# A planner that lets GpSimd and VectorE's SBUF-only operations take turns

## The chip, the cores and the metric

The kernel runs on one core of one Trainium2 chip. The core has five engines with a queue of instructions each: TensorE (PE in the profile, its weight loads PEld), VectorE (DVE), ScalarE (ACT), GpSimd (POOL) and SyncE (SP), from whose queue all DMAs of this kernel are issued. Each engine works through its own queue in order; between engines there are only semaphores. The metric is device time in microseconds (us) of one execution; less is better.

## The reference

A delta-rule linear attention over 4 batches, 8 heads, 768 positions and head width 48, and behind it a gated MLP with a mix over the sequence:

```python
k_n = k / (np.linalg.norm(k, axis=-1, keepdims=True) + 1e-06)
for t in range(S):
    y[:, :, t] = einsum('bhd,bhde->bhe', q[:, :, t], state)
    v_old = einsum('bhde,bhd->bhe', state, k_n[:, :, t])
    state += beta_t * outer(k_n[:, :, t], v[:, :, t] - v_old)
...
h = relu(x @ w_in); u, v = halves of h        # x: 4 x 768 x 384, d_ff 1024
v_n = (v - mean(v)) / sqrt(var(v) + 1e-06)
v_s = w_spatial @ v_n + b_spatial
out = (u * v_s) @ w_out
```

Some weights of the MLP arrive as 64-bit floats and are taken apart into 32-bit words on the chip.

## The kernel before, in words

**The work.** The sequence is cut into chunks of 64 positions; 4 batches of 12 chunks make 48 *steps*. A step computes, for four pairs of heads at a time, in matmuls of 64 rows or fewer (the "tiles", all issued at L438): `a` (state times keys), `b` (the chunk's triangular inverse times the corrected values, whose result VectorE scales into the tile `us`, L795), `c` (the state's update, added at L823), `qk` (masked at L839) and `d` (the output, copied out by ScalarE at L868). Each step's `b` needs the step before it of the same batch.

Steps come in 12 groups of four. For a group, `norm` makes the coefficients `cn` from the keys' squares (VectorE, L557 to L583), `mask` scales a mask by them (GpSimd, L595; on VectorE for two chunks), `kk` makes the triangular matrices (VectorE L630 into `ta`), a DMA through DRAM puts them into another layout (`ad`, `la`), and `lanes` inverts 32x32 blocks with 60 VectorE operations (L670 and L677, on the tile `pw` in PSUM) before another DMA brings them back; `step_t` and `step_ef` put the blocks together. The first group goes a shorter way, `lanes16` (L1181, L1188, all in SBUF).

**The MLP.** When four steps of a batch are done, `convert` splits their output into a high and a low part for fp32r matmuls: ScalarE writes `xh` (L911), GpSimd or, late in the kernel, VectorE subtracts to get `xl` (L915). Then follow the tasks `v` (L946), `u` (L1012), `g` (L1044, the mix over the sequence) and `o` (L1099) on TensorE with their work on the other engines; `vl` (L992) and `gl` (L1086) are low parts as `xl` is. `post_v` has six small VectorE operations on the tile `sm` (helper `small`, L963 to L983).

**The weights.** `load_w` loads a piece of a weight, and where it holds 64-bit floats six VectorE operations on SBUF (L467 to L483, tile `wstage` or `ub`) and one on GpSimd (L485) make 32-bit floats of it; ScalarE (L487) and GpSimd (L489) make the high and the low part. The pieces of `w_in` are needed before the first `v`, those of `w_spatial` and `w_out` before the first `g`.

**What sets the order.** Every engine's queue is written by a planner, the class `Line`, while the kernel is built. Every job is a generator that yields one operation at a time: an engine, how long it holds that engine (`occ`), when its result is there (`lat`), a condition, and a due time. `step` collects the operations that can begin, finds the earliest, takes those of the same engine that could begin almost as early (within `SLACK`), and emits the one whose due time is first. VectorE's costs come from `dve`, GpSimd's from `pool`. Where TensorE would stand still in the plan, `keep_warm` puts in filler matmuls (L1282, tile `ones`), and `tensor` lets two tile operations of different kinds (the kinds "anti" and "diag") run interleaved in one *round*; a round with no partner is run alone, or beside a filler on the tile `mpos`. So a changed cost or condition in the planner can change every queue of the program, and the count of fillers and lone rounds with it. The planner's times are used nowhere on the chip: what holds an instruction there is its place in the queue, its semaphores, and the hardware.

## Time and profile before

| | us |
|---|---|
| median of 3 executions (range) | 556.83 (556.48 to 558.57) |
| the profiled execution, its own time | 559.02 |
| its span, first to last instruction | 557.3 |
| TensorE busy | 509.1 (91%) |
| VectorE busy | 355.2 (64%) |
| ScalarE busy | 216.9 (39%) |
| GpSimd busy | 140.7 (25%) |
| mean granted TensorE clock | 0.941 |

Lines (L...) are those of the kernel before. A row of the timeline gives start, duration, engine, line, operation, the tile written and the tiles read, shapes and count; in brackets how long the engine had nothing to do before, and who ended that. A row of the chain of waits gives start, duration and what the chain stands in. Matmul times are modelled as pipelined, so that TensorE's share is no share of its peak; fillers count as busy.

### The profile page before, as it was taken

To read this page: it belongs to the slowest core of one execution; us is meant where nothing else is said; L and a number is where in the kernel's file an instruction comes from. 1 tells how busy PE (TensorE), PEld (TensorE's weight loads), DVE (VectorE), ACT (ScalarE), POOL (GpSimd) and SP (SyncE) were. 2 spreads that over 40 slices of the span, in tenths; PEclk is the share of its full clock that TensorE was granted. 3 is DMA by queue.
4 is the path that set the end of the run, shared out by engine and by line. 5 is a ranking of instruction groups with operands and counts; after the bars stand their busy time and mean duration, and the time that the engine had idled before them with its cause. 6 is when DMAs were issued, how large, how long until landed. Compare 5 with 4: busy or idle time off the path is not lost.

```text
span 557.3 us, 22530 instructions
## 1 busy us (share of the span) xinstructions
PE 509.1 (91%) x9605; PEld 460.0 (83%) x9605; DVE 355.2 (64%) x1436; ACT 216.9 (39%) x536; POOL 140.7 (25%) x210
## 2 busy tenths in 40 slices
PE   5965797978979999899999999999999999999997
PEld 5855786867867879798987789989987999999997
DVE  4899978776977988478989894683135241134210
ACT  3222524544625535242235465422165441137111
POOL 5525224555425441402314252310001000000000
PEclk9777586897999999899999999999999999999999
DMA  8688378495759754786875727343014010100011
GB/s 241 163 179 163 88 186 220 113 259 104 181 158 191 187 135 91 177 219 146 204 133 79 204 73 173 112 142 62 29 35 133 8 36 29 35 18 16 1 42 44
DMA packets 134256, 67.03 MB, mean 120 GB/s; under 512 B 105894, under 2 KB 123532, under 8 KB 134156
## 3 DMA queue, kind: packets, MB, share of 16 engines
q1 hardware_dynamic: 134156, 65.60, 47.8%
q8 instruction: 75, 1.23, 0.9%
q14 instruction: 25, 0.20, 0.1%
HBM read 50.11 MB, written 15.17 MB: 117 GB/s over the span
## 4 chain that ended last, share of the span: by engine, by line
PE 65%; DVE 16%; DMA 7%; issue 4%; ACT 3%; SPq 3%; POOL 0%; DVEq 0%; ACTq 0%
PE pt L438 22%; PE pm L1044 12%; PE pw L1044 6%; PE pm L1012 6%; PE pm L946 5%; PE pm L1099 5%; PE pw L1099 3%; DVE prod L670 3%; DVE pw L677 3%; DMA kv<-in_kv_t 2%; DMA la<-ad 2%; PE pm L1282 2%; PE pw L946 2%; PE pw L1012 1%; DMA ad<-ta 1%
## 5 line engine op out<-in xcount | busy, mean ns | idle before, releaser
L670 DVE TENSOR_TENSOR prod<-pw,la 128x96 f32<-128x96 f32 (+10 forms) x330 | 78.3, 241 | 13.4 <-ACT pw L664 8.8
L677 DVE TENSOR_TENSOR pw<-pw,prod 128x96 f32<-128x96 f32 (+9 forms) x330 | 81.1, 249 | 4.6
L719 POOL TENSOR_TENSOR kv<-kv,cn 128x192 f32<-128x192 f32 x48 | 24.9, 519 | 159.4 <-DMA kv<-in_kv_t 93.1
L1044 PE MATMUL pm<-wsp_h,vh 128*128 128x256 f32 x192 | 57.0, 297 | 0.0
L1044 PE MATMUL pm<-wsp_l,vh 128*128 128x256 f32 x192 | 54.2, 282 | 0.6 <-issue 0.6
L1044 PE MATMUL pm<-wsp_h,vl 128*128 128x256 f32 x192 | 54.0, 281 | 0.0
L438 PE MATMUL pt<-kv,st 48*64 48x64 f32 x768 | 53.8, 232 | 0.0
L438 PE MATMUL pt<-aq,us 64*64 64x64 f32 x768 | 52.0, 227 | 0.8 <-issue 0.8
L438 PEld LDWEIGHTS pt<-kv,st 48*64 48x64 f32 x768 | 43.3, 142 | 3.2 <-DVE ta L630 1.5
L1080 ACT CAST gh<-tmp 128x512 fp32r<-128x512 f32 x24 | 14.8, 619 | 76.0 <-DVE tmp L1061 76.0
L438 PEld LDWEIGHTS pt<-aq,us 64*64 64x64 f32 x768 | 43.5, 142 | 1.0 <-issue 1.0
L1282 PE MATMUL pm<-ones 128*128 128x256 f32 x215 | 40.6, 339 | 3.2 <-ACT ones L282 2.5
L438 PE MATMUL pt<-ta,pi 64*64 64x32 f32 x768 | 36.2, 235 | 5.1 <-issue 3.9
L595 POOL TENSOR_TENSOR mc<-mpos,cn 128x256 f32<-128x256 f32 x46 | 28.3, 628 | 43.1 <-DVE cn L583 24.8
L438 PE MATMUL pt<-kv 48*64 48x64 f32 x768 | 36.0, 233 | 3.2 <-issue 2.2
L438 PEld LDWEIGHTS pt<-kv,ta 64*64 64x64 f32 x768 | 30.2, 145 | 9.8 <-issue 3.2
L438 PEld LDWEIGHTS pt<-st,kv 48*64 48x64 f32 x704 | 26.9, 141 | 13.8 <-issue 3.7
L1282 PEld LDWEIGHTS pm<-ones 128*128 128x128 f32 x215 | 33.8, 231 | 5.3 <-ACT ones L282 2.5
L868 ACT ACTIVATE xs<-pt 112x256 f32<-112x256 f32 x48 | 18.3, 381 | 50.7 <-PE pt L438 40.1
L1044 PEld LDWEIGHTS pm<-wsp_h,vh 128*128 128x128 f32 x192 | 36.4, 190 | 1.6
L438 PE MATMUL pt<-kv,ta 64*64 64x48 f32 x768 | 35.9, 233 | 1.9 <-DVE kv L779 0.5
L1044 PEld LDWEIGHTS pm<-wsp_h,vl 128*128 128x128 f32 x192 | 36.6, 190 | 0.6 <-issue 0.6
(182 smaller groups left out, 1488.2 us busy)
## 6 DMA issues: line engine op xcount, KB each, us to landing
kv<-in_kv_t SPq DMA_DIRECT2D x48, 456.0 KB, 4.5
ad<-ta SPq DMA_DIRECT2D x24, 256.0 KB, 4.5
la<-ad SPq DMA_DIRECT2D x44, 128.0 KB, 4.1
out<-ob SPq DMA_DIRECT2D x24, 192.0 KB, 1.9
k<-in_kv_t SPq DMA_DIRECT2D x20, 224.0 KB, 3.6
knn<-in_k_nat SPq DMA_DIRECT2D x10, 384.0 KB, 3.9
wd<-w SPq DMA_DIRECT2D x22, 128.0 KB, 3.9
ta<-wd SPq DMA_DIRECT2D x44, 64.0 KB, 3.5
```

The lines of the kernel that those rows point to most:

```text
L438: return lambda: nc.tensor.matmul(*a, **dict(dict(start=True, stop=True), **k))
L595: (nc.vector if t in (0, 2) else nc.gpsimd).tensor_tensor(out=mc, in0=mall, in1=cns[t // G][:, t % G, 1].unsqueeze(2).broadcast_to([128, N ...
L670: nc.vector.tensor_tensor(out=pr, in0=w[:, :n, j : j + 1].broadcast_to([128, n, m]), in1=la[:, j, j + 1 : 32].unsqueeze(1).broadcast_to([1 ...
L677: nc.vector.tensor_add(out=w[:, :n, j + 1 : 32], in0=w[:, :n, j + 1 : 32], in1=pr)
L719: nc.gpsimd.tensor_tensor(out=v, in0=v, in1=cns[s // G][:, s % G, 0].unsqueeze(2).broadcast_to([128, NU, HD]), op=ALU.mult)
L868: nc.scalar.mul(out=xt[0:112, :, qt * 64 : qt * 64 + 64], in_=psl(held[0][1], CH)[0:112], mul=-1.0)
L946: nc.tensor.matmul(p[1], a[:, kt, ts], w[:, kt, DH:], start=(n == 0), stop=(n == 3 * NK - 1))
L1012: nc.tensor.matmul(pu[:, k], w[:, kt, d0 : d0 + 128], a[:, kt], start=(n == 0), stop=(n == 3 * NK - 1))
L1044: nc.tensor.matmul(pg[:, k], v[:, d0 : d0 + 128], w[:, si, ts], start=(n == 0), stop=False)
L1080: nc.scalar.copy(out=gh[:, hs], in_=gt)
L1099: nc.tensor.matmul(p[1][:, :DM], a[:, dd, ts], w[:, dd], start=(n == 0), stop=(n == 3 * ND - 1))
L1282: nc.tensor.matmul(free[0].rearrange("p (n t) -> p n t", t=128), ones, ones.unsqueeze(1).broadcast_to([128, 2, 128]), start=True, stop=True,)
```

## The change

The planner gets two more clocks, `held["DVE"]` and `held["POOL"]`. A VectorE operation made by the new helper `dve_sb` is of the kind "port". In the plan such an operation does not begin before the last planned GpSimd operation has ended, and no GpSimd operation begins before the last planned "port" operation has ended. All other VectorE operations are planned as before. No instruction gets a new wait on the chip, none moves to another engine; VectorE has 1436 instructions in both versions, ScalarE's, GpSimd's and SyncE's counts are the same too, and TensorE's differ by fillers alone.

```diff
@@ class Line
+        self.held = {"DVE": 0.0, "POOL": 0.0}
...
             if t is not None:
-                found.append((max(self.t[op.eng], t), op, j, t))
+                e = max(self.t[op.eng], t)
+                if op.eng == "POOL":
+                    e = max(e, self.held["DVE"])
+                elif op.kind == "port":
+                    e = max(e, self.held["POOL"])
+                found.append((e, op, j, t))
...
         t, op, j, _ = min(near, key=lambda f: (f[1].due(), f[0]))
+        t = self.port(op, t)
         self.t[eng] = t + op.occ
         self.grant(j, t + op.lat)
+
+    def port(self, op, t):
+
+        if op.eng == "POOL":
+            t = max(t, self.held["DVE"])
+            self.held["POOL"] = t + op.occ
+        elif op.kind == "port":
+            t = max(t, self.held["POOL"])
+            self.held["DVE"] = t + op.occ
+        return t
...
+def dve_sb(dep, due, e, fast=1.0):
+
+    op = dve(dep, due, e, fast)
+    op.kind = "port"
+    return op
...
-            t = yield dve(on(t), d, n, 0.5)
+            t = yield dve_sb(on(t), d, n, 0.5)
             nc.vector.tensor_scalar(
                 out=e, in0=w1, scalar1=20, scalar2=0x7FF, op0=ALU.logical_shift_right, op1=ALU.bitwise_and
             )
```

The same replacement of `dve` by `dve_sb` is made for all six operations of `load_w`, for the square at L557 and L569, L573, L575, L577, L581, L583 of `norm` (not for its sums and reciprocals), for the two masks on VectorE (L595), for `lanes16` (L1181, L1188, L1190) and for L1254. The operations of `small`, `xl`, `vl` and `gl` where VectorE does them, and everything that reads or writes PSUM stay `dve`.

Lines behind the new code stand 24 higher in the changed file. Three places show what the new plan makes of the queues.

VectorE's queue around the fifth step's `us` (L795; L819 in the changed file), where `norm` makes the coefficients of the fifth group. Before:

```order
L795 TENSOR_TENSOR us<-pt,cs 128x192
L562 TENSOR_REDUCE ss<-knn 128x8
L670 TENSOR_TENSOR prod<-pw,la 128x120
L569 TENSOR_SCALAR t<-nr 128x16
L677 TENSOR_TENSOR pw<-pw,prod 128x10x12
L571 RECIPROCAL t<-t 128x16
```

And in the changed program, where that step's `us` is the instruction 33 places ahead of L593:

```order
L847 TENSOR_TENSOR st<-st,pt 112x192
L701 TENSOR_TENSOR pw<-pw,prod 128x13x6
L701 TENSOR_TENSOR pw<-pw,prod 128x2x27
L694 TENSOR_TENSOR prod<-pw,la 128x65
L593 TENSOR_SCALAR t<-nr 128x16
L701 TENSOR_TENSOR pw<-pw,prod 128x13x5
L595 RECIPROCAL t<-t 128x16
```

The first of the coefficient operations (L569, now L593) stood three instructions behind the fifth step's `us` and now stands 33 behind it.

VectorE's queue around the tenth step's `us`. Before:

```order
L677 TENSOR_TENSOR pw<-pw,prod 128x15
L779 TENSOR_TENSOR kv<-kv,pt 128x192
L682 MEMSET pw 64x16
L839 TENSOR_TENSOR aq<-pt,mpos 128x256
L682 MEMSET pw 64x16
L467 TENSOR_SCALAR wstage<-wstage 128x256
L471 TENSOR_SCALAR wstage<-wstage 128x256
L795 TENSOR_TENSOR us<-pt,cs 128x192
L473 TENSOR_SCALAR wstage<-wstage 128x256
```

And now:

```order
L701 TENSOR_TENSOR pw<-pw,prod 128x15
L819 TENSOR_TENSOR us<-pt,cs 128x192
L706 MEMSET pw 64x16
L863 TENSOR_TENSOR aq<-pt,mpos 128x256
L706 MEMSET pw 64x16
L847 TENSOR_TENSOR st<-st,pt 112x192
L605 TENSOR_TENSOR t<-nr,ball 128x16
L863 TENSOR_TENSOR aq<-pt,mpos 128x256
L607 SCALAR_TENSOR_TENSOR cn<-t,nr 128x4x4
L491 TENSOR_SCALAR wstage<-wstage 128x128
L491 TENSOR_SCALAR wstage<-wstage 128x256
```

Two operations on a weight piece (L467 and L471; L491 and L495 now) stood ahead of the step's `us`; now they stand behind it and behind the state's update.

TensorE's queue around the tenth step, with buffer numbers; a row that ends in x8 is a round of eight small matmuls with no partner, and alternating rows are a round of two operations. Before:

```order
L438 MATMUL pt1_204<-ta2_179,pi0_91 64x32 x8
L438 MATMUL pt2_205<-st1_110,kv0_167 64x48
L438 MATMUL pt3_206<-ta2_179,pi1_92 64x32
...
L438 MATMUL pt0_203<-kv1_168 64x64 x8
L1282 MATMUL pm0_207<-ones_67 128x256 x6
```

And now:

```order
L462 MATMUL pt2_205<-ta2_179,pi0_91 64x32 x8
L462 MATMUL pt0_203<-kv0_167 64x64 x8
L462 MATMUL pt1_204<-st1_110,kv0_167 64x48
L462 MATMUL pt3_206<-tn1_176,ta2_179 64x32
...
L462 MATMUL pt2_205<-kv1_168 64x64 x8
L1306 MATMUL pm0_207<-ones_67 128x256
L462 MATMUL pt0_203<-ta2_179,pi1_92 64x32 x8
L462 MATMUL pt3_206<-kv0_167,ta2_179 64x48 x8
```

The last block product of the group (`ta2,pi1`) shared a round with the state's update (`st1,kv0`) and now runs alone, as do two more. Over the whole program there are 236 rounds before and 239 now; those of eight matmuls with no partner are 60 before and 70 now. Filler matmuls on `ones` are 253 before and 247 now, those on `mpos` 232 and 200.

More of the change, by code (lines that the diff above doesn't have):

```diff
@@ L469, in load_w @@
             )
-            t = yield dve(on(t), d, n, 0.5)
+            t = yield dve_sb(on(t), d, n, 0.5)
             nc.vector.tensor_scalar(out=e, in0=e, scalar1=896.0, scalar2=1150.0, op0=ALU.max, op1=ALU.min)
-            t = yield dve(on(t), d, n, 0.5)
+            t = yield dve_sb(on(t), d, n, 0.5)
             nc.vector.tensor_scalar(
@@ L475, in load_w @@
             )
-            t = yield dve(on(t), d, n)
+            t = yield dve_sb(on(t), d, n)
             nc.vector.scalar_tensor_tensor(
@@ L555, in norm @@
             if g == 0:
-                t = yield dve(on(t), d, n)
+                t = yield dve_sb(on(t), d, n)
                 nc.vector.tensor_mul(out=kp, in0=kp, in1=kp)
@@ L567, in norm @@
         n3 = nr.rearrange("p (s u) -> p s u", u=NU)
-        t = yield dve(on(t), d, 16)
+        t = yield dve_sb(on(t), d, 16)
         nc.vector.tensor_scalar_max(out=t0, in0=nr, scalar1=1e-30)
@@ L571, in norm @@
         nc.vector.reciprocal(out=t0, in_=t0)
-        t = yield dve(on(t), d, 16)
+        t = yield dve_sb(on(t), d, 16)
         nc.vector.tensor_mul(out=t0, in0=t0, in1=ss)
-        t = yield dve(on(t), d, 16)
+        t = yield dve_sb(on(t), d, 16)
         nc.vector.tensor_add(out=t0, in0=t0, in1=nr)
-        t = yield dve(on(t), d, 16)
+        t = yield dve_sb(on(t), d, 16)
         nc.vector.tensor_scalar(out=cn[:, :, 0], in0=t3, scalar1=0.5, scalar2=EPS, op0=ALU.mult, op1=ALU.add)
@@ L579, in norm @@
         nc.vector.reciprocal(out=n3, in_=cn[:, :, 0])
-        t = yield dve(on(t), d, 16)
+        t = yield dve_sb(on(t), d, 16)
         nc.vector.tensor_mul(out=t3, in0=n3, in1=bn)
-        t = yield dve(on(t), d, 16)
+        t = yield dve_sb(on(t), d, 16)
         nc.vector.scalar_tensor_tensor(out=cn[:, :, 1], in0=t3, scalar=-1.0, in1=n3, op0=ALU.mult, op1=ALU.mult)
@@ L593, in mask @@
         dep = at(("cn", t // G), ("kk", t - 2) if t >= 2 else None)
-        x = yield dve(dep, d, 256) if t in (0, 2) else pool(dep, d, 256)
+        x = yield dve_sb(dep, d, 256) if t in (0, 2) else pool(dep, d, 256)
         (nc.vector if t in (0, 2) else nc.gpsimd).tensor_tensor(
@@ L1179, in lanes16 @@
             pr = pt[:, : j * m].rearrange("p (a b) -> p a b", b=m)
-            t = yield dve(on(t), d, j * m)
+            t = yield dve_sb(on(t), d, j * m)
             nc.vector.tensor_tensor(
@@ L1186, in lanes16 @@
             )
-            t = yield dve(on(t), d, j * m)
+            t = yield dve_sb(on(t), d, j * m)
             nc.vector.tensor_add(out=w[:, :j, j + 1 : 16], in0=w[:, :j, j + 1 : 16], in1=pr)
-        t = yield dve(on(t), d, 16)
+        t = yield dve_sb(on(t), d, 16)
         nc.vector.memset(w.rearrange("p i t -> p (i t)")[:, 0:256:17], 1.0)
@@ L1252, in load_bias @@
         nc.scalar.copy(out=brow[r], in_=x[r])
-        t = yield dve(on(t), due(4), 256)
+        t = yield dve_sb(on(t), due(4), 256)
         nc.vector.scalar_tensor_tensor(
```

4 lines of the change are left out of this document (2 added, 2 removed).

## The prediction

> **What bounds the kernel now.** I first read the busy times in four stretches.
>
> ```profile
> core 0: us, PE busy (x) PEld busy (x) DVE busy (x) ACT busy (x) POOL busy (x), PEclk, DMA share, GB/s
> 0.00:63.00 63.00, 43.11 (x964) 39.41 (x966) 52.52 (x194) 20.92 (x59) 27.74 (x69) 0.77 0.74 172
> 63.00:200.00 137.00, 120.47 (x2953) 104.60 (x2951) 110.74 (x500) 62.42 (x163) 61.44 (x77) 0.88 0.70 174
> 200.00:380.00 180.00, 172.65 (x3814) 153.62 (x3815) 141.08 (x611) 74.45 (x184) 48.98 (x60) 0.99 0.61 144
> 380.00:557.30 177.30, 172.91 (x1883) 162.39 (x1881) 50.84 (x134) 59.14 (x132) 2.53 (x5) 1.00 0.12 36
> ```
>
> From 200 us on TensorE is busy for 345.6 of 357.3 us, at a full clock: there the end moves only with TensorE's own work. Before 200 us TensorE is idle for 36.4 us, part of the rest is fillers, and VectorE is busy for 163.3 of 200 us (82%). So time can be won before 200 us, on VectorE's queue and on the waits between engines, and what is won there shifts the TensorE-bound part forward. GpSimd is busy for 89.2 us of these 200, so it is often in the way if it can be in the way at all. Whether it can, two places of the timeline show.
>
> ```profile
> 90.84 0.36 DVE L795 TENSOR_TENSOR us<-pt,cs 128x192 f32<-128x192 f32 x1
> 93.96 1.81 POOL L915 TENSOR_TENSOR xl<-xs,xh 128x768 fp32r<-128x768 f32 x1 [3.37 <-ACT xh L911]
> 94.29 1.52 DVE L569 TENSOR_SCALAR t<-nr 128x16 f32<-128x16 f32 x1 [2.45 <-ACT nr L564]
> 96.84 0.17 DVE L577 TENSOR_SCALAR cn<-t 128x16 f32<-128x16 f32 x1
> ...
> 133.21 1.83 POOL L915 TENSOR_TENSOR xl<-xs,xh 128x768 fp32r<-128x768 f32 x1 [2.91 <-ACT xh L911]
> 134.34 0.85 DVE L467 TENSOR_SCALAR wstage<-wstage 128x256 uint32<-128x256 uint32 x1
> 135.73 0.34 DVE L795 TENSOR_TENSOR us<-pt,cs 128x192 f32<-128x192 f32 x1
> 136.46 0.42 DVE L477 SCALAR_TENSOR_TENSOR wstage<-wstage 128x256 uint32<-128x256 uint32 x1
> ...
> 19.98 0.28 DVE L481 TENSOR_SCALAR wstage<-wstage 128x256 uint32<-128x256 uint32 x1
> ```
>
> L569 works on 16 elements, for which its like (L577) takes 0.17 us. It took 1.52 us and ended at 95.81, just behind GpSimd's subtraction, which ended at 95.77. L467 at 134.34 took 0.85 us where an undisturbed operation of that size takes 0.28 (L481), and the `us` of the tenth step stood behind it. So a VectorE operation on SBUF that finds a GpSimd operation under way waits for its end, with everything queued behind it. How much that is in all, the groups by shape show.
>
> ```profile
> L569 DVE TENSOR_SCALAR t<-nr 128x16 f32<-128x16 f32 x12 | 5.4, 448 | 3.1 <-ACT nr L564 2.7
> L467 DVE TENSOR_SCALAR wstage<-wstage 128x256 uint32<-128x256 uint32 x14 | 5.7, 410 | 0.5 <-DMA wstage<-in_w_in 0.5
> L477 DVE SCALAR_TENSOR_TENSOR wstage<-wstage 128x256 uint32<-128x256 uint32 x14 | 7.1, 510 | 0.0
> L481 DVE TENSOR_SCALAR wstage<-wstage 128x256 uint32<-128x256 uint32 x14 | 5.5, 395 | 0.0
> L471 DVE TENSOR_SCALAR wstage<-wstage 128x256 uint32<-128x256 uint32 x14 | 4.9, 352 | 0.1
> L977 DVE SCALAR_TENSOR_TENSOR sm<-sm 128x1 f32<-128x1 f32 x24 | 6.5, 272 | 0.4
> L983 DVE TENSOR_TENSOR sm<-sm 128x1 f32<-128x1 f32 x24 | 5.9, 248 | 0.4
> L630 DVE TENSOR_TENSOR ta<-pt,mc 128x256 f32<-128x256 f32 x48 | 19.7, 414 | 2.4 <-PE pt L438 1.6
> ```
>
> L569 lost 12 x (448 - 170) = 3.3 us, L467 14 x (410 - 280) = 1.8, L477 14 x (510 - 420) = 1.3, L481 1.6 and L471 1.0 in the same way. Counted instruction by instruction (VectorE beside a running GpSimd instruction, more than 60 ns over the usual time of its own shape) 52 instructions lost 20.8 us. Of that 17.2 us fell on operations that the change marks as "port", and 3.6 on L977 and L983, which it doesn't mark. L630, which reads PSUM, took 414 ns with GpSimd at work or not.
>
> Last, which of these losses stand on the chain of waits:
>
> ```profile
> 23.11 0.82 DVE wstage L481
> 94.29 1.52 DVE t L569
> 134.34 0.86 DVE wstage L467
> 146.32 1.09 DVE wstage L467
> 151.61 0.74 DVE wstage L481
> 274.01 1.08 DVE t L569
> 301.15 1.63 DVE sm L983
> 305.48 0.80 DVE sm L977
> ```
>
> These eight hold 0.54, 1.35, 0.57, 0.81, 0.46, 0.9, 1.5 and 0.6 us of loss. With the shorter ones, 30 delayed instructions stand on the chain (the first one at 22.50, the last is the row at 305.48). They lost 12.7 us there: 10.2 on marked operations, of which 9.2 lie before 200 us, and 2.5 on L977 and L983.
>
> **The change, part by part.** *Removed stalls.* No instruction goes away; what can go away are the marked losses on the chain. The upper bound is 10.2 us. The lower bound is nothing: the chip doesn't enforce the plan's turns, and GpSimd begins when its own inputs are there (the two `xl` above were released by ScalarE). Two places can be followed. L569 of the fifth group stood 3 instructions behind the fifth step's `us` and now stands 33 behind; at 0.24 us each (the rows below) that is some 7 us later. The `us` began at 90.84, 4.9 us before `xl` ended, so L569 now comes after `xl`, and 1.35 us on the chain go away. At the tenth step L467 now stands behind `us`, so that a stall there would no longer hold up the recurrence (0.57 us). Both would then come from the planner's knowing; for the other places the plan must be right to about a microsecond in when ScalarE or a DMA releases GpSimd. I take half of 10.2: 5.1 us won.
>
> [...]
>
> *Added TensorE rounds.* There are three more rounds. The price is in these rows of the chain, a round of eight alone (16 records) and one with a partner:
>
> ```profile
> 404.68 0.58 PE pt L438 x16
> 425.40 0.62 PE pt L438 x31
> ```
>
> A lone round costs as much as a shared one, so 3 x 0.6 = 1.8 us, if all fall where TensorE bounds. If they fall before 200 us into idle time they cost nothing. I take 1.8.
>
> *Fillers.* There are 6 fewer on `ones` and 32 fewer on `mpos`. They stand in planned gaps, and those on `mpos` beside a round that runs anyway: 0, and at most 6 x 0.34 = 2 us less by the group of all fillers:
>
> ```profile
> L1282 PE MATMUL pm<-ones 128*128 128x256 f32 x215 | 40.6, 339 | 3.2 <-ACT ones L282 2.5
> ```
>
> *Moved VectorE work.* The first step's `us` stood at place 193 of VectorE's queue and now stands at 218. The 25 operations put ahead of it are mostly of `lanes`:
>
> ```profile
> 62.93 0.35 DVE L795 TENSOR_TENSOR us<-pt,cs 128x192 f32<-128x192 f32 x1
> L677 DVE TENSOR_TENSOR pw<-pw,prod 128x96 f32<-128x96 f32 (+9 forms) x330 | 81.1, 249 | 4.6
> L670 DVE TENSOR_TENSOR prod<-pw,la 128x96 f32<-128x96 f32 (+10 forms) x330 | 78.3, 241 | 13.4 <-ACT pw L664 8.8
> ```
>
> At 0.245 us each this is 6.1 us of work ahead of the `us` that began at 62.93. It is only moved: the fifth step's `us` stands at place 286 instead of 289, the twelfth's at 481 instead of 502, the sixteenth's at 570 instead of 605. The nineteenth's stands at 770 instead of 695, but there MLP work went ahead of it on TensorE too (292 instead of 184 of the MLP's matmuls stand before its `b`), in a stretch that TensorE fills. I take 0 for it, with 0 to 6.1 us slower as bounds: the cover is the same work, later needed; if the first steps are really late and the first MLP tasks with them, it is paid.
>
> GpSimd's and SyncE's queues are reordered as well. GpSimd had 111 of 200 us free before the TensorE-bound part, and TensorE's waits name it once:
>
> ```profile
> PE pt L438 <- POOL kv L719: 0.4, 1, 0.4
> 32.77 4.10 DMA la<-ad
> ```
>
> So 0 for it. What is late next where a stall goes is the way through DRAM (`ad` and `la`) behind the group's matrices, in which the chain stands already (4.1 us in the second row): one more reason to take half.
>
> *Sum.* -5.1 + 1.8 = -3.3 us against the profiled execution's 559.02 (span 557.3 and 1.7 around it), so 555.7. The median of the three runs, 556.83, lies 2.2 lower; the same sum gives 553.5.
>
> **The rivals.** *A, the forecast:* a quarter to three quarters of the 10.2 us go away, with the rounds: 550.9 to 556.1, middle 553.5.
>
> *B, the collisions only move:* for it speaks that GpSimd's start hangs on other engines and that no wait is added; against it that two large collisions are moved by 7 us or out of the path. Then only the rounds are left: 558.6.
>
> *C, slower: the first steps come late and the lead is not made up.* The place is VectorE's queue ahead of the first `us`. The price is 6.1 us of work, with 1.8 for the rounds, less 2 of stalls: 556.8 + 5.9 = 562.7. For it speaks that VectorE is busy for 52.5 of the first 63 us, so that work put ahead is not free; against it that 8.3 of the 20.8 us of loss lie before 63 us, and that by the fifth step fewer operations stand ahead than before. It decides if the fourth step's `us`, at 81.7 before, begins later than 84.5.
>
> *D, nearly all marked losses on the chain go:* 556.8 - 10.2 + 1.8 = 548.4. For it speaks that losses in a queue in order add up; against it that the waits behind them (DMA, TensorE) are not shortened with them.
>
> **How the numbers follow.** A 38%, B 25%, C 22%, D 15%. What a measurement of this kernel can tell from no change is about 0.5%, 2.8 us: faster is below 554.0, slower above 559.6. A gives 30 faster and 8 same; B 2 faster, 18 same, 5 slower; C 2 same, 20 slower; D 15 faster. Together 47% faster, 28% same, 25% slower. The predicted time is A's, 553.5, with 550.9 to 556.1 as its own range. The range for 8 in 10 goes from 546 (D with 2 us of fillers) to 563 (C).
>
> **What would show it.** In the changed profile the means of L467, L481 and L569 (24 lines further down) should fall towards 280, 280 and 170 ns; half of the way is the forecast, no fall is B. L977's and L983's should stay as they are, and L630's at 414. The fourth step's `us` should begin before 82. TensorE's idle time before 200 us should shrink from 36 us by 3 to 5. It would be wrong if the losses fall and the end stays, which would mean that the chain's VectorE part was only a stand-in for another wait, or if a new wait of several us stands in TensorE's first 200 us.

## The result, and the profile after

The change makes the kernel slower: 574.89 us (median of 4 executions, 572.78 to 578.29) against 557.7 (4 executions, 556.48 to 561.71) beside it, a ratio of 1.028 with a 95% interval of 1.023 to 1.033. The forecast was 553.5. A second comparison, made later beside other executions of the kernel before, gave 576.4 against 563.9, with a ratio of 1.012 (1.005 to 1.020). The ratios leave out executions more than 1.5% above the fastest of their kernel, so a ratio need not be the quotient of two medians; this matters most for the change with the planned cost of 0.076 us, below, of whose ten executions six are left out (0.999 without them, 1.006 by the medians of all).

First the four stretches of the changed kernel, with the columns that the prediction showed of before:

```profile
core 0: us, PE busy (x) PEld busy (x) DVE busy (x) ACT busy (x) POOL busy (x), PEclk, DMA share, GB/s
0.00:63.00 63.00, 38.00 (x912) 35.12 (x912) 49.57 (x202) 20.61 (x58) 28.11 (x71) 0.75 0.73 172
63.00:200.00 137.00, 117.01 (x2642) 103.00 (x2646) 103.48 (x461) 59.69 (x152) 56.89 (x69) 0.85 0.68 167
200.00:380.00 180.00, 170.82 (x3665) 150.72 (x3661) 133.14 (x584) 73.79 (x184) 49.91 (x63) 0.96 0.57 133
380.00:575.10 195.10, 189.88 (x2340) 176.67 (x2331) 66.01 (x192) 64.15 (x145) 4.56 (x9) 1.00 0.16 47
```

TensorE is busy for 515.7 of 575.1 us, so idle for 59.4; before it was 48.1 of 557.3. Its busy time times what the granted clock lacks to 1.00 (38.0 x 0.25 + 117.0 x 0.15 + 170.8 x 0.04) makes 33.9 us lost to a slower clock; the rows of before give 26.1. Both are estimates that take TensorE's pace to go with the granted clock. What is left is work at full clock: 481.8 now, 483.0 before. So the 17.8 us are 11.3 of idle TensorE, 7.8 of slower clock, and 1.2 less work. No added work made it slower: TensorE waited more, and its mean granted clock was 0.922, before 0.941.

The losses that the change was to take away did get smaller where they are marked. The groups of the changed kernel by shape (the coefficient operations and two that have no mark at the end):

```profile
L593 DVE TENSOR_SCALAR t<-nr 128x16 f32<-128x16 f32 x12 | 2.5, 206 | 0.4 <-ACT nr L588 0.3
L491 DVE TENSOR_SCALAR wstage<-wstage 128x256 uint32<-128x256 uint32 x14 | 4.5, 318 | 1.0 <-DMA wstage<-in_w_in 1.0
L501 DVE SCALAR_TENSOR_TENSOR wstage<-wstage 128x256 uint32<-128x256 uint32 x14 | 6.3, 452 | 0.1
L505 DVE TENSOR_SCALAR wstage<-wstage 128x256 uint32<-128x256 uint32 x14 | 4.4, 314 | 0.0
L597 DVE TENSOR_TENSOR t<-t,ss 128x16 f32<-128x16 f32 x12 | 3.6, 301 | 0.1
L601 DVE TENSOR_SCALAR cn<-t 128x16 f32<-128x16 f32 x12 | 3.7, 305 | 0.0
L607 DVE SCALAR_TENSOR_TENSOR cn<-t,nr 128x16 f32<-128x16 f32 x12 | 3.7, 305 | 0.1
L1001 DVE SCALAR_TENSOR_TENSOR sm<-sm 128x1 f32<-128x1 f32 x24 | 7.8, 327 | 0.5
L1007 DVE TENSOR_TENSOR sm<-sm 128x1 f32<-128x1 f32 x24 | 6.5, 272 | 0.4
```

And the same three coefficient operations before:

```profile
L573 DVE TENSOR_TENSOR t<-t,ss 128x16 f32<-128x16 f32 x12 | 2.9, 238 | 0.0
L577 DVE TENSOR_SCALAR cn<-t 128x16 f32<-128x16 f32 x12 | 2.0, 167 | 0.1
L583 DVE SCALAR_TENSOR_TENSOR cn<-t,nr 128x16 f32<-128x16 f32 x12 | 2.6, 215 | 0.2
```

L569 went from 448 to 206 ns, L467 from 410 to 318, L481 from 395 to 314 and L477 from 510 to 452, but L573, L577 and L583 rose by 63, 138 and 90, and the unmarked L977 and L983 from 272 and 248 to 327 and 272. Counted instruction by instruction as in the prediction, 38 instructions lose 18.1 us, against 52 and 20.8 before; on marked operations the loss fell from 17.2 to about 12.5, on unmarked ones it rose from 3.6 to about 5.6. On the chain of waits the loss is 13.0 us, against 12.7. Its longest pieces now are these (start, duration, what the chain stands in):

```profile
105.78 1.75 DVE cn L601
147.12 1.06 DVE sm L1001
187.88 1.00 DVE t L597
311.77 1.63 DVE sm L1007
316.00 0.90 DVE sm L1001
```

One place shows how a collision moved. This is the timeline of VectorE and GpSimd in the changed kernel around the coefficients of the fifth group, whose norm ScalarE had ready at 98.8:

```profile
104.68 0.16 DVE L593 TENSOR_SCALAR t<-nr 128x16 f32<-128x16 f32 x1
105.45 0.16 DVE L599 TENSOR_TENSOR t<-t,nr 128x16 f32<-128x16 f32 x1
105.64 3.67 POOL L513 TENSOR_TENSOR wsp_l<-wstage,wsp_h 128x768 fp32r<-128x768 f32 x2 [3.78 <-ACT wsp_h L511]
105.69 1.83 DVE L601 TENSOR_SCALAR cn<-t 128x16 f32<-128x16 f32 x1
107.56 0.25 DVE L603 RECIPROCAL nr<-cn 128x16 f32<-128x16 f32 x1
112.03 0.17 DVE L605 TENSOR_TENSOR t<-nr,ball 128x16 f32<-128x16 f32 x1
112.42 0.17 DVE L607 SCALAR_TENSOR_TENSOR cn<-t,nr 128x16 f32<-128x16 f32 x1
```

L593 no longer meets GpSimd and takes 0.16 us (before 1.52). L601 of the same chain meets it instead, for 1.83 us: GpSimd, released by ScalarE, had begun 0.05 us ahead of it. And the eight operations, which took from 94.29 to 97.95 before, now begin at 104.68 and end at 112.59: they stand 37 places apart in VectorE's queue, where they stood 14 apart.

What became of that is seen where TensorE waits for the group's inverse, in the first of its `tn` (count, durations in ns, first and last start). Before:

```profile
L734 DVE STREAM_TRANSPOSE tn<-ta x4: 269/296/301, 183.7 to 185.9; 128x128 f32<-128x128 f32 x4
```

And in the changed kernel, with TensorE's waits from 190 to 215 us behind it:

```profile
L758 DVE STREAM_TRANSPOSE tn<-ta x4: 271/308/311, 198.4 to 200.8; 128x128 f32<-128x128 f32 x4
...
PE pt L462 <- DVE tn L758: 3.5, 1, 3.5
```

The inverse comes 14.7 us later. Until then TensorE had kept up: its useful work (all matmuls but the fillers, each at its time at full clock) was 0.2 us behind the kernel before at 180 us. At 200 us it was 6.3 behind, at 220 it was 12.5, at 240 it was 8.8, at 300 it was 10.5 and at 400 it was 15.0. (How a matmul is weighed moves single values by up to 4 us; the jump from 180 to 220 us stays.) What the granted clock was around the wait, slices of 5 us show, in the changed kernel:

```profile
190.00:195.00 5.00, 3.60 (x20) 2.61 (x18) 4.59 (x22) 1.49 (x3) 2.62 (x2) 1.00 0.90 237
195.00:200.00 5.00, 1.49 (x48) 1.25 (x50) 4.72 (x23) 0.48 (x2) 2.34 (x4) 0.86 0.78 111
200.00:205.00 5.00, 5.00 (x52) 3.78 (x47) 3.00 (x13) 2.98 (x10) 2.33 (x5) 0.50 0.32 58
205.00:210.00 5.00, 5.00 (x96) 3.94 (x98) 3.05 (x18) 3.26 (x9) 0.00 (x0) 0.50 0.01 3
210.00:215.00 5.00, 4.94 (x154) 4.52 (x149) 3.05 (x19) 2.17 (x7) 1.98 (x3) 0.78 0.33 97
```

TensorE is idle for 4.9 us from 190 to 200, and then runs for about 12 us at a granted clock of 0.50, which costs another 6.1 by the same estimate (5.0 x 0.5 + 5.0 x 0.5 + 4.94 x 0.22). That may be too much: by the profile's modelled ends the 128x512 matmuls of L970 took 0.63 us there (median) and 0.39 at a clock of 1.00 (172 to 195 us), 1.6 times as long and not twice. Before, the clock was 1.00 in all five slices.

The step that the third rival (C, first steps late) named was late, and made up again. The `us` of the first, fourth, sixteenth and seventeenth step in the changed kernel:

```profile
67.62 0.36 DVE L819 TENSOR_TENSOR us<-pt,cs 128x192 f32<-128x192 f32 x1 [0.81 <-PE pt L462]
...
87.46 0.36 DVE L819 TENSOR_TENSOR us<-pt,cs 128x192 f32<-128x192 f32 x1 [0.49 <-PE pt L462]
...
180.59 0.34 DVE L819 TENSOR_TENSOR us<-pt,cs 128x192 f32<-128x192 f32 x1
207.35 0.36 DVE L819 TENSOR_TENSOR us<-pt,cs 128x192 f32<-128x192 f32 x1 [1.51 <-PE pt L462]
```

The last two before:

```profile
179.97 0.36 DVE L795 TENSOR_TENSOR us<-pt,cs 128x192 f32<-128x192 f32 x1
189.14 0.34 DVE L795 TENSOR_TENSOR us<-pt,cs 128x192 f32<-128x192 f32 x1
```

The first and the fourth are 4.7 and 5.8 us late, the sixteenth 0.6, the seventeenth 18.2.

### The profile page after: what moved, and what is told of

Same layout as the page of the kernel before. It is cut to its first block, busy times and chain, and to the rows that moved or that the text cites. A ratio compares the mean times of both kernels' runs of the same rounds, so it can differ in the third digit from the quotient of the medians.

```text
span 575.1 us, 22387 instructions
## 1 busy us (share of the span) xinstructions
PE 515.7 (90%) x9535; PEld 465.5 (81%) x9535; DVE 352.2 (61%) x1436; ACT 218.2 (38%) x536; POOL 139.5 (24%) x210
## 4 chain that ended last, share of the span: by engine, by line
PE 68%; DVE 12%; DMA 7%; ACT 4%; issue 4%; SPq 4%; POOL 0%; DVEq 0%; ACTq 0%
PE pt L462 25%; PE pm L1068 12%; PE pw L1068 6%; PE pm L1036 6%; PE pm L1123 5%; PE pm L970 4%; PE pm L1306 3%; PE pw L1123 3%; DMA kv<-in_kv_t 2%; DVE prod L694 2%; SPq L678 1%; DVE pw L701 1%; PE pw L970 1%; PE pw L1036 1%; DMA knn<-in_k_nat 1%
## 5 line engine op out<-in xcount | busy, mean ns | idle before, releaser
L694 DVE TENSOR_TENSOR prod<-pw,la 128x96 f32<-128x96 f32 (+8 forms) x330 | 77.6, 242 | 11.8 <-ACT pw L688 7.5
L701 DVE TENSOR_TENSOR pw<-pw,prod 128x96 f32<-128x96 f32 (+10 forms) x330 | 80.1, 250 | 4.3
L1306 PE MATMUL pm<-ones 128*128 128x256 f32 x247 | 48.9, 345 | 2.5 <-ACT ones L306 2.5
L1306 PEld LDWEIGHTS pm<-ones 128*128 128x128 f32 x247 | 40.2, 236 | 5.2 <-ACT ones L306 2.5
L462 PE MATMUL pt<-kv,ta 64*64 64x48 f32 x768 | 37.1, 235 | 5.9 <-issue 1.9
L619 POOL TENSOR_TENSOR mc<-mpos,cn 128x256 f32<-128x256 f32 x46 | 28.3, 625 | 57.7 <-DVE ta L654 34.0
L462 PEld LDWEIGHTS pt<-kv,ta 64*64 64x64 f32 x768 | 31.0, 147 | 12.9 <-issue 4.9
L462 PE MATMUL pt<-k 48*64 48x64 f32 x640 | 30.8, 243 | 10.7 <-DVE ub L1212 6.2
L462 PE MATMUL pt<-kv 48*64 48x64 f32 x768 | 37.4, 239 | 2.6 <-DMA kv<-in_kv_t 2.0
L462 PEld LDWEIGHTS pt<-us,kv 64*64 64x64 f32 x704 | 27.6, 145 | 13.7 <-DVE us L819 5.3
L462 PE MATMUL pt<-tn,ta 64*64 64x32 f32 x768 | 35.3, 235 | 3.7 <-DVE tn L758 3.5
```

The lines of the kernel that those rows point to most:

```text
L462: return lambda: nc.tensor.matmul(*a, **dict(dict(start=True, stop=True), **k))
L619: (nc.vector if t in (0, 2) else nc.gpsimd).tensor_tensor(out=mc, in0=mall, in1=cns[t // G][:, t % G, 1].unsqueeze(2).broadcast_to([128, N ...
L694: nc.vector.tensor_tensor(out=pr, in0=w[:, :n, j : j + 1].broadcast_to([128, n, m]), in1=la[:, j, j + 1 : 32].unsqueeze(1).broadcast_to([1 ...
L701: nc.vector.tensor_add(out=w[:, :n, j + 1 : 32], in0=w[:, :n, j + 1 : 32], in1=pr)
L1306: nc.tensor.matmul(free[0].rearrange("p (n t) -> p n t", t=128), ones, ones.unsqueeze(1).broadcast_to([128, 2, 128]), start=True, stop=True,)
```

## The experiments

A *deal* is one filling of the queues by the planner, and "with the port" means a plan with the change's rule. The theories, as the expectations name them. **T**: marked coefficient operations starve in the plan (any other VectorE operation that can begin at once is emitted ahead of them while GpSimd holds the port), so the inverses of some groups come late, and that is the loss. **R**: the late first steps are the loss, or the collisions that moved. **N**: the order of before is a favourable draw, and any other deal of the same instructions costs 1 to 3%, with the port in the plan or without. **M** is, in the fifth to eighth run, that taking turns loses by itself whatever is marked; in the last two it is that a deal costs by how late the inverses come. **K**: half of the loss is the clock that falls behind a wait.

T fitted the profile best, and the first four runs were made for it.

**The coefficients of the fifth group alone unmarked.**

```diff
 # norm, six times
-t = yield dve_sb(on(t), d, 16)
+t = yield (dve if g == 4 else dve_sb)(on(t), d, 16)
```

> The changed kernel, but the eight coefficient operations of the fifth group alone are planned as plain VectorE work; all other marked operations still take turns with GpSimd. In the changed profile TensorE's useful work is level with before until 180 us and 12 us behind at 220 us, while it waits for the fifth group's inverse; that group's last coefficient came at 112.6 us instead of 97.9. Theory T (the turns starve the chain of eight coefficient operations, that chain carries one group's whole preparation): the last coefficient comes back to about 98 to 101 us, the fifth group's first transpose from 198 to 184 to 188 us, and 10 to 13 us of the 17 go away: 561 to 566 us. Rival R (the first steps' late start and the moved collisions cost the time): nothing of that is undone, so 572 to 578. Rival N (any re-dealing of the queues costs as much, whichever group is touched): no tie to this group, 565 to 580.

Measured: 1.032 (1.024 to 1.041), no gain over the change, and the end missed what T forecast. Locally it went T's way: the fifth group's coefficients were done at 101.4 (112.6 in the change), its first `tn` came at 190.0 (T: 184 to 188), and TensorE was 6.4 us behind at 220 and not 12.5. But the ninth group's `tn` was then 33 us late and the end 14.6. The loss moved on to another group.

**All of `norm` unmarked, the other marks kept.**

```diff
 # norm
-t = yield dve_sb(on(t), d, 16)
+t = yield dve(on(t), d, 16)
```

> The changed kernel with all of the coefficient work of every group planned as plain VectorE work; the weight pieces, the first group's short inverse and the rest still take turns. T: no group's coefficients are stretched, 555 to 563 us. R: the first step's place in VectorE's queue stays late (the 224th instruction, 194th before), so 570 to 578. N: 565 to 580.

Measured: 1.004 (0.999 to 1.010). The first steps are late here too (first `us` at 71.2), so R is out as the cause.

**The kernel before, with the fifth group's coefficients held back until the sixth step's `us`.**

```diff
 # norm
-t = yield dve(on(t), d, 16)
+t = yield dve(both(on(t), at(("U", 5))) if g == 4 else on(t), d, 16)
```

> The kernel before, no turns at all; the fifth group's coefficient chain is only held in the plan until the sixth step's scaled tile is done, which puts its first operation 43 instructions further back in VectorE's queue. T: the last coefficient comes near 110 us instead of 98, the fifth group's steps are late by 10 to 14 us and the time is 566 to 572. R: no collision rule, first step as before: 555 to 560. N: 560 to 575.

Measured: 1.033 (1.027 to 1.040), more than expected. Its first `tn` came at 201.9, 18.2 us late. Holding one group back, without any port, can cost as much as the change does. But the edit deals all later work anew as well (five subtractions went from VectorE to GpSimd with it), so the cost isn't shown to be the late inverse's alone.

**Only `norm` marked.** All other marks are taken back.

> The kernel before with turns for the coefficient operations alone; the weight pieces and the first group's inverse are planned as before, and the first step stands where it stood before. T: the fifth group's eight operations are spread over 55 places of VectorE's queue (15 before, 38 in the changed kernel), so 568 to 578 us. R: 555 to 560, as the first steps are not late. N: 560 to 575.

Measured: 1.032 (1.025 to 1.040). TensorE was only 1.5 us behind at 220 and lost 10 of its 15 us between 220 and 300. The first `us` came at 63.7 (62.9 before), so this run too speaks against R. So far T held in what it said of `norm`, but not in where the loss stands.

**Only the weights marked.** The marks of `norm`, `mask`, `lanes16` and `load_bias` are taken back.

> Only the weights' operations (load_w) keep the mark; norm, mask, lanes16 and load_bias are as before. The eight coefficient operations of every group stay within 8 to 20 places of VectorE's queue, as before. Theory T (the loss is that marked coefficient operations of norm starve in the plan, so that the inverses of some groups come late): within 1% of before, 0.995 to 1.01. Rival M (taking turns at the port loses by itself, whatever operations are marked): most operations marked are still marked, so half of the loss or more stays, 1.015 or more. If the turns win what the prediction had counted for the weights' losses on the chain, up to 1% faster.

Measured: 1.011 (1.000 to 1.023): between T's bound and M's.

**Another deal without the port.**

```diff
 # dve() of the kernel before: the planned latency
-0.2 + 0.00104 * e * fast
+0.205 + 0.00104 * e * fast
```

> The kernel before, with the planned latency of a VectorE operation at 0.205 us in place of 0.2: no port in the plan, the same instructions, but dealt differently (the first step's us at place 209 to 217 of VectorE's queue as in the change, the sixteenth's at 695 where the kernel before has 605), with the coefficient operations close together as before. Theory T: within 1% of before. Rival N (the plan of before is the best of many drawn and any other deal costs 2 to 3%): 1.02 or more. Rival R (late first steps cost): about 1.01.

Measured: 1.012 (1.006 to 1.017). Up to the ninth group no inverse is late here by more than 1.0 us, most are early, and it still costs about 1%. That is a little more than T's 1% and less than N's 2%; it is R's "about 1.01", but R has failed in the second and fourth run. It is the first loss without the port.

**The port known, but operations chosen by due time.**

```diff
 # Line.step of the change
-elif op.kind == "port":
-    e = max(e, self.held["POOL"])
```

> All marks stay and the plan knows the port, but a VectorE operation is chosen by its due time as before, and only then made to wait for GpSimd in the plan's time (the queue stands behind it, as on the chip). No operation can starve: the coefficient operations stay within 8 to 17 places, those of the fifth group stand at 286 to 301 (before 293 to 307, the change 320 to 357). Theory T: the loss goes, 0.99 to 1.01. Rival M (turns at the port lose by themselves): 1.015 or more.

Measured: 1.031 (1.025 to 1.037). T fails: the coefficients stand close together and in time, and the loss is all there. In this deal the third group's `tn` comes 12.6 us late and every later one 14 to 28. M's 1.015 or more is met here, and in the next run.

**The port one-sided.** As in the run before, and `port` makes only GpSimd wait.

```diff
 # Line.port
 elif op.kind == "port":
-    t = max(t, self.held["POOL"])
     self.held["DVE"] = t + op.occ
```

> All marks stay, but in the plan only GpSimd waits for VectorE's marked operations, never the other way round. The coefficient operations stay within 8 to 17 places, those of the fifth group stand at 285 to 299. Theory T: the loss goes, 0.99 to 1.01. Rival M: 1.015 or more. Against the run in which VectorE is made to wait after the choice by due time, T has no difference of more than 1%.

Measured: 1.017 (1.011 to 1.023). T's 0.99 to 1.01 fails here too.

**Fillers for the wait for the fifth group's `tn`.** In TensorE's queue 28 more matmuls on `ones` stand ahead of the seventeenth step's first round; nothing else differs.

> The change, with 28 more fillers (matmuls on ones) in TensorE's queue just ahead of the seventeenth step's first round, where TensorE waited 3.5 us for tn (195.2 to 198.75); nothing else in any queue differs. 20 such fillers took 2.65 us shortly before, so 28 fit into the wait. Theory K (half of the loss is the granted clock, which falls behind a wait: 0.50, 0.50 and 0.78 in the three slices from 200 to 215 us): the clock there stays at 0.9 or more, TensorE's lag behind before at 220 us falls from 12.5 to 6 to 8 us, and the end comes 3 to 6 us earlier than the change's: ratio 1.018 to 1.023 to before. Rival (the clock there falls for another reason, or the end waits for VectorE anyway): clock as before, or the end within 1 us of the change's.

> The change itself, beside the run with the fillers on the same chip: 1.025 to 1.032 of before.

The timeline and the 5 us slices of the run with the fillers:

```profile
199.52 3.63 PE L1309 MATMUL pm<-ones 128*128 128x256 f32 x29
203.09 0.24 PE L464 MATMUL pt<-tn,ta 64*64 64x32 f32 x1
...
200.00:205.00 5.00, 5.00 (x94) 4.70 (x93) 4.90 (x23) 1.49 (x4) 2.63 (x5) 1.00 0.65 95
205.00:210.00 5.00, 5.00 (x138) 3.87 (x136) 4.45 (x26) 4.49 (x14) 1.65 (x4) 1.00 0.32 61
210.00:215.00 5.00, 4.83 (x173) 4.32 (x169) 4.81 (x31) 3.47 (x11) 1.99 (x3) 1.00 0.43 119
```

The fillers filled the wait and the clock stayed at 1.00. But the ratios are 1.015 (1.008 to 1.022) with them and 1.012 (1.005 to 1.020) for the change itself, the medians 573.87 and 576.4: no gain that can be told, and both are lower than was expected of them. In the profile of this run TensorE was 4.2 us behind already at 180 us, and 11.0 at 220: it lost 6.8 us between, where the first profile of the change lost 12.3. K is right about the clock of the slices, and not shown for the end.

**The tenth group's coefficients held back in the kernel before.** As for the fifth group above, until the 28th step's `us`; this group has 33 us to spare.

> The kernel before, with the coefficient operations of the tenth group held back until the 28th step's us (264.2 before; they began at 249.3), the same edit that cost 3.3% on the fifth group. The tenth group's tn came at 322.6 and its first us at 356.1, so there are some 33 us to spare. Theory T (a late inverse costs only where TensorE then waits for it): 0.995 to 1.012. Rival N (any operation held back spoils the whole plan): 1.02 or more.

Measured: 1.010 (1.002 to 1.018), within T's range and below N's. The same edit costs 3.3% on a group whose inverse TensorE waits for, and 1% here. As both edits deal later work anew too, the difference need not be the late inverse's alone.

**Another deal, at 0.080 us.**

```diff
 # dve() of the kernel before: the planned occupancy
-0.078 + 0.00104 * e * fast
+0.080 + 0.00104 * e * fast
```

> The kernel before, with the planned occupancy of a VectorE operation at 0.080 us in place of 0.078: another deal of the same instructions, with coefficient operations within 8 to 17 places, the fifth group's at 305 to 319 (before 293 to 307). The first such deal cost 1.2%. Theory T: 0.99 to 1.015, by which group comes late; rival N (the plan of before is a lucky draw): 1.01 to 1.03.

Measured: 1.024 (1.016 to 1.031): without the port nearly all of what the change costs. Its fifth group's `tn` came 12.3 us late.

**Deals in pairs, with and without the port.** The planned occupancy of a VectorE operation at 0.076 us, in the kernel before and in the change; at 0.080 us in the change; and at 0.082 us in the kernel before.

> The kernel before with the planned occupancy of a VectorE operation at 0.076 us (0.078 before): a third deal without the port. Theory T (marked coefficient operations starve in the plan, and that is the loss): 0.99 to 1.012. Rival N (any other deal of this plan costs, with the port or without): 1.01 to 1.03, as the deals at 0.205 us of latency (1.012) and at 0.080 us (1.024).

> The change with the same 0.076 us. The coefficient operations of the fifth and eighth groups spread over 39 and 38 places. T: 1.5 to 3% slower than the deal at 0.076 us without the port. N: within 1% of it, either way.

> The change with 0.080 us. The coefficient operations of the fifth group spread over 26 places and begin at 343 (the deal at 0.080 us without the port: 14 places, 305). T: 1.5 to 3% slower than that deal, so 1.04 to 1.055 of before. N: within 1% of that deal's 1.024.

> The kernel before with 0.082 us: a fourth deal without the port, in which the first step's us and the fifth group's coefficient operations stand where they stood before (193 and 292 to 306, before 194 and 293 to 307), and later work is dealt otherwise. T: 0.99 to 1.012. N: 1.01 to 1.03.

Measured: at 0.076 us 1.036 (1.027 to 1.045) without the port and 0.999 (0.992 to 1.007) with it; at 0.080 us 1.037 (1.028 to 1.046) with it, against 1.024 without; at 0.082 us 1.028 (1.019 to 1.038) without. The stretches of the change at 0.076 us up to 380 us:

```profile
0.00:63.00 63.00, 38.96 (x895) 35.66 (x897) 48.78 (x198) 19.48 (x51) 27.05 (x68) 0.81 0.70 172
63.00:200.00 137.00, 118.70 (x2892) 101.22 (x2891) 116.45 (x537) 70.59 (x184) 63.63 (x79) 0.90 0.68 173
200.00:380.00 180.00, 171.11 (x3852) 151.12 (x3845) 136.65 (x569) 68.51 (x170) 46.75 (x59) 0.98 0.62 146
```

Here VectorE did 165.2 us of work in the first 200 us (153.1 in the change, 163.3 before), with the coefficients of the fifth and eighth groups spread over 39 and 38 places. Those of the fifth were done at 110.8, 12.9 us later than before, yet its first `tn` came only 4.4 us late. So T falls: a plan with every mark and with spread coefficients loses nothing that can be told. With it falls M, that taking turns loses by itself. The port is 3.7 points better at 0.076 us, 1 to 3 worse at 0.078, and 1.3 worse at 0.080, where the intervals overlap. N had forecast less than 1% between the two plans of a pair, and that failed as well. What stands of N is its broad form: any other deal can cost 1 to 3.6%, and the sign of what the port does was not the same in every deal.

**All preparation of the fifth and later groups due one step earlier,** in the change and in the kernel before (`norm`, `mask`, `kk`, `bounce`, `load_la`, `lanes`):

```diff
 # lanes; the others alike
-d = due(4 * g - 3.5)
+d = due(4 * g - 3.5 - (1 if g > 3 else 0))
```

> The change, with everything that prepares the inverses of the fifth and later groups (norm, mask, kk, bounce, load_la, lanes) due one step earlier in the plan. The coefficient operations of the fifth group stay spread as in the change (320 to 357), and the seventeenth step's us comes back from place 680 to 645 (before 650). Theory M (a deal costs by how late the inverses come and TensorE waits for them, whatever made them late): the inverses of groups 5 to 7 come within 6 us of before, and the time falls to 1.00 to 1.012. Rival N in its strict form (any other deal costs the same 1 to 3.5%, not to be steered): 1.02 or more.

> The kernel before with the same earlier due times, without the port. M: inverses no later than before, 0.99 to 1.01. Strict N: 1.01 to 1.035. A port that helps by the stalls it takes away would show as the run with the port being up to 1% faster than this one.

Measured: 1.019 (1.012 to 1.025) with the port, 1.021 (1.014 to 1.029) without. With the port the inverses came back as M said, the fifth group's here:

```profile
L758 DVE STREAM_TRANSPOSE tn<-ta x4: 290/296/302, 186.6 to 189.5; 128x128 f32<-128x128 f32 x4
```

That is 2.9 us behind before (14.7 in the change), and the sixth and seventh groups' are 3.7 behind and 7.0 ahead. But the time did not follow (M: at most 1.012), so M in this simple form fails as well: the ninth group's `tn` was then 13.1 us late. In this plan, moving the preparation forward only moved what is late. The strict N is met without the port and just missed with it (1.02 or more), and the 0.3% by which the run with the port is faster lies within the intervals.

All runs together (for the run with only the weights marked the columns of the profile are left out). Idle and clock loss are TensorE's, the latter summed over slices of 5 us; with the work at full clock they make the span of the profiled execution. Late is the mean over the fifth to ninth groups of how much later than before the first `tn` came; stalls are VectorE's losses beside a running GpSimd.

| run | ratio (95%) | span | idle | clock loss | work | late | stalls |
|---|---|---|---|---|---|---|---|
| before | 1 | 557.3 | 48.1 | 26.0 | 483.2 | 0 | 20.8 |
| the change | 1.028 (1.023 to 1.033) | 575.1 | 59.4 | 35.2 | 480.5 | 12.0 | 18.1 |
| the change again | 1.012 (1.005 to 1.020) | 568.0 | 60.4 | 25.0 | 482.6 | 8.1 | 16.6 |
| with fillers | 1.015 (1.008 to 1.022) | 572.9 | 56.4 | 33.7 | 482.8 | 12.0 | 15.9 |
| port, 0.076 | 0.999 (0.992 to 1.007) | 556.3 | 56.6 | 21.2 | 478.5 | -2.2 | 18.8 |
| port, 0.080 | 1.037 (1.028 to 1.046) | 573.7 | 60.7 | 38.6 | 474.3 | 10.2 | 11.5 |
| port, early | 1.019 (1.012 to 1.025) | 566.7 | 60.0 | 20.8 | 485.9 | 3.7 | 15.0 |
| no port, 0.205 latency | 1.012 (1.006 to 1.017) | 562.8 | 58.2 | 25.5 | 479.0 | -6.7 | 20.6 |
| no port, 0.076 | 1.036 (1.027 to 1.045) | 572.6 | 57.7 | 33.1 | 481.8 | 7.5 | 26.3 |
| no port, 0.080 | 1.024 (1.016 to 1.031) | 579.3 | 55.1 | 39.4 | 484.9 | 13.0 | 19.7 |
| no port, 0.082 | 1.028 (1.019 to 1.038) | 572.2 | 57.1 | 32.3 | 482.8 | 6.6 | 23.3 |
| no port, early | 1.021 (1.014 to 1.029) | 567.6 | 55.6 | 28.0 | 484.0 | 3.5 | 23.0 |
| no port, fifth group held | 1.033 (1.027 to 1.040) | 577.1 | 60.3 | 40.4 | 476.4 | 11.4 | 22.6 |
| no port, tenth group held | 1.010 (1.002 to 1.018) | 566.7 | 48.1 | 32.6 | 486.0 | 1.4 | 21.2 |
| fifth group free | 1.032 (1.024 to 1.041) | 571.9 | 58.5 | 29.9 | 483.5 | 9.3 | 13.2 |
| `norm` free | 1.004 (0.999 to 1.010) | 564.0 | 51.1 | 22.4 | 490.4 | -0.9 | 13.6 |
| only `norm` | 1.032 (1.025 to 1.040) | 572.4 | 59.2 | 33.6 | 479.6 | 9.0 | 21.4 |
| only the weights | 1.011 (1.000 to 1.023) | | | | | | |
| chosen by due time | 1.031 (1.025 to 1.037) | 578.7 | 60.0 | 32.4 | 486.4 | 23.0 | 20.3 |
| one-sided | 1.017 (1.011 to 1.023) | 569.2 | 51.2 | 34.4 | 483.6 | 10.6 | 22.9 |

Three things are read from it. First, the five deals without the port in which nothing was held back cost 1.2, 3.6, 2.4, 2.8 and 2.1%, 2.4 in the mean. The four plans with the change's rule and all its marks cost 2.0 (mean of the change's two comparisons), -0.1, 3.7 and 1.9%, 1.9 in the mean. The two sets can't be told apart. The intervals are those of one comparison each, and the change's two comparisons differ by 1.6 points, so the single values are less sure than they look. Second, the rule does what it says to the stalls: 15.0 to 18.8 us, once 11.5, against 19.7 to 26.3 in the eight plans without the port, about 6 us less in the mean (16.0 and 22.2). But stalls and span have a correlation of 0.06 over the 19 profiles. Third, the spans go with idle and clock loss together (0.88; what is left of a span is work, 474 to 490 us) and with the lateness of the inverses (0.86). That these groups set the time is not shown by it, since whatever delays the program delays them too, and putting three of them in time did not mend it.

No version is faster than the kernel before: `norm` free and the port at 0.076 us are level with it.

## Why the prediction was wrong

*The step that failed* is "Moved VectorE work", where I took "0 for it, with 0 to 6.1 us slower as bounds". I priced what the new plan moves by the 25 operations ahead of the first `us`, took the cover to be "the same work, later needed", and was right about that place: the first step came 4.7 us late, the fourth met C's condition (87.5, later than 84.5), and by the sixteenth step 0.6 us were left. But the new plan deals all five queues anew, far behind that place too. What such a deal is worth was measured without the port at 1.2 to 3.6%, 6.7 to 20 us (of the batches' medians of 561 to 564), three times my upper bound; nothing in the rows of before bounds it. The change adds nothing to that which these runs can tell.

A premise went with it: "there the end moves only with TensorE's own work", of the time from 200 us on. By the four stretches TensorE's idle time grew by 8.6 us before 200 us and by 2.7 behind it, and its loss to the clock by 2.7 and 5.1. So 7.8 us were lost in the part where nothing but work was to count.

*The removed stalls, -5.1 us.* Half of the 10.2 us on the chain were to go. All stalls fell from 20.8 to 18.1 us, those on the chain rose from 12.7 to 13.0: nothing of it was won on the path. The rule does lower the total, by some 6 us over several deals, so the mechanism of the forecast is there; in this plan nothing of it reached the path. Counted in much the same way on the chains of all profiles, the losses are about 6 to 13 us in the six with the rule and 7 to 18 in the eight without: less by about 4 us in the mean, with ranges that overlap.

*The 33 places of L569* were counted as 1.35 us won. The operation did miss its collision, and a later one of the same chain, the fourth behind it, met the next. That is rival B's mechanism: L601 began 0.05 us behind GpSimd and took 1.83 us, its usual time being 0.17. The prediction's sentence that a VectorE operation on SBUF waits for a GpSimd operation under way is too wide: the reciprocal L603 of the same chain began at 107.56, beside the second of GpSimd's two subtractions (107.5 to 109.3), and took 0.25 us, where all twelve of its line took 0.23 to 0.25. What I had not asked is what the 33 places do to the chain behind them: L569 began 10.4 us later (I had 7), and the coefficients of that group were done 14.6 us later.

*Added rounds, +1.8.* There are three more, but TensorE's work at full clock fell by 1.2 to 2.7 us, by the two ways of cutting slices, in a program with 38 fewer fillers. The term can't be told apart in that.

*GpSimd's and SyncE's queues, 0.* Nothing in the runs speaks against it by itself; a deal moves them too, and they were not tried apart.

*Rivals.* B was right about the stalls on the chain and 16 us too fast about the end (558.6). C was right about the sign and its condition, and wrong about the place: its 6.1 us were made up. D is out. Of the signs named, the means of L467, L481 and L569 went 70, 70 and 87% of the way to 280, 280 and 170 ns, more than the half that was forecast, and L630's (L654 now) stayed at 415; L977's and L983's rose. TensorE's idle time before 200 us grew from 36.4 to 45.0 where it was to shrink by 3 to 5. Both signs that were to refute the forecast came: the marked losses fell and the end did not follow, and a new wait of several us (3.5 for `tn`) stands in the first 200 us.

*What stays open.* Which property of a deal sets its time. Late inverses go with it, a plan in which one group was held back cost 3.3%, and the loss stands in TensorE's waits and the clock behind them; but mending the fifth group, its clock or all the later groups' due times each left 1 to 3%. Why the order of before is better than nearly all its neighbours isn't shown by its profile, and whether it is merely the best of many that were drawn no run here tests.

## What to carry to other kernels

Where a planner writes the queues, measure first what an unrelated nudge of a planned cost does to the time, two or three of them; here a change of 3% in one number cost up to 3.6%, and a gain below that can't be read from one plan with the change and one without. Judge such a rule by what it does to the thing that it is for (the stalls, here a quarter less) and by several deals each, and price a moved operation by the chain that hangs on it, not by its own duration.

## What the runs showed of the hardware

In two profiles of the changed kernel a wait of TensorE was followed by work at a granted clock near 0.50, for 12 us in one and for less than 6 in the other. In the first, 4.9 us of idle time within 10 us were followed by this (slices of 2 us):

```profile
204.00:206.00 2.00, 2.00 (x17) 1.38 (x15) 0.71 (x5) 0.95 (x3) 0.00 (x0) 0.50 0.00 0
210.00:212.00 2.00, 2.00 (x39) 1.88 (x34) 0.84 (x6) 0.97 (x4) 1.48 (x2) 0.50 0.51 117
212.00:214.00 2.00, 1.94 (x77) 1.70 (x78) 1.51 (x11) 0.93 (x4) 0.51 (x1) 0.94 0.29 117
```

And in the second profile of the same program, where TensorE waited 5.4 us ahead of the same matmuls, which began at 197.3:

```profile
201.00:203.00 2.00, 2.00 (x19) 1.25 (x18) 1.07 (x5) 0.79 (x3) 0.83 (x2) 0.52 0.22 73
203.00:205.00 2.00, 2.00 (x44) 1.49 (x40) 1.00 (x7) 1.20 (x5) 0.00 (x0) 1.00 0.00 0
```

In the first profile TensorE was busy in every slice from 200 to 212 us, by the profile's modelled ends, and the granted clock stayed at 0.50 for these 12 us. In the second it was back at 1.00 within 6 us of the first matmul. A mix of rounds of 64-row matmuls and MLP work ran in both stretches, from the same queue, so the mix alone doesn't decide how long the clock stays down; what does was not tried. With 28 fillers in the wait the slices from 200 to 215 us had a clock of 1.00.

Two executions of one program also differ by more than I had taken: the change gave 569.8 to 581.0 us on one chip, and its two profiles have spans of 575.1 and 568.0 with 35.2 and 25.0 us of clock loss at nearly the same idle time (59.4 and 60.4). The 0.5% that the prediction took as a measurement's limit was too small for single plans compared once.
